# A Fourier-mixing and feed-forward kernel: three of the second batch's folds moved to GpSimd, and the last chunk's closing additions rearranged

## The chip, the cores and the metric

The kernel runs on one core of a Trainium2 chip. A core has a matrix engine (TensorE, "PE" in the profile, with its weight loads listed apart as "PEld"), an elementwise engine (VectorE, "DVE"), an activation engine (ScalarE, "ACT"), a programmable engine (GpSimd, "POOL") and a queue that issues transfers (SyncE, "SP"). The engines run side by side[...]. The metric is the time on the device in microseconds (us) of one execution, given as the median of several.

## The reference

```
X = fft(fft(x, axis=1), axis=2).real         # x: 8 batches x 3008 rows x 256 columns, f32
h = X.reshape(24064, 256) @ w_in             # 256 -> 2048
g = maximum(0.01 * h, h)                     # leaky ReLU
out = g @ w_out                              # 2048 -> 256
```

So a real part of a two-dimensional Fourier transform is taken for each of eight batches, and every one of its 24,064 rows then passes through a feed-forward layer with a leaky ReLU between its two matrices.

## The kernel before

**The Fourier part.** The transform along the 3008 rows is a matrix product with tables of cosines and sines, made small by folding: rows that the tables treat alike are added to or subtracted from one another first. The transform along the 256 columns is merged into the first matrix of the layer. The folds of a batch's `x` are `folds_of_x` (line 399) and `fold_halves_of_x` (line 413): elementwise additions in the tile `xt`. Of batch 1, `folds_of_x(0)` makes eight; then, on another part of the batch, `folds_of_x(1)` makes eight more and `fold_halves_of_x` the last eight. They are not run at once. They go into a queue (`Later`, line 937) and are let out one by one between the pieces of the matrix work.

**Folds by turns.** `by_turns` (line 952) treats every second fold alike. One of two first has ScalarE copy an operand to a PSUM bank (`dft_ps`, line 958), and VectorE then adds SBUF and PSUM (line 948). The other is an addition with both operands in SBUF, on VectorE as well (line 950); it alone is put on a list named `gate`. The next GpSimd addition waits for the last entry of that list (`wait_for_gate`, line 994). The additions of two SBUF results in `make` (line 1180) are put on it too.

**The layer.** After two pieces done in a plain way, the columns are worked in 31 chunks; the last of them, like most, has 376 columns in two halves of 188. For each chunk `up` (line 1094) makes 16 blocks of hidden values: two matmuls each, a ScalarE copy (line 1103), two VectorE operations (line 1110), and the leaky ReLU on ScalarE (line 1364 in the profile). The second matrix is applied by a fast matrix multiplication: 28 additions of hidden blocks (`sum`, line 1122, the operations of line 1127, 18 of them on GpSimd and 10 on VectorE), 26 block products (`product`, line 1133, the matmuls of line 1144), which gather in 24 sums numbered 0 to 23, and 34 additions of those sums (`make`, the operations of line 1188, all on VectorE) that give eight results. Each result is stored at once by `put` (line 1210, transfers of line 1213 on SP's queue).

**Banks.** The 24 sums of a chunk lie two to a PSUM bank, sum `a` in bank `a // 2`, and the banks rotate through three tiles, `sum_psa`, `sum_psb` and `sum_psc`. A bank is handed to `combine` (line 1153) when its second sum is complete. Sums listed in `COPIED` are copied to SBUF by ScalarE (line 1160); the others stay in PSUM until a `make` has read them. Before a bank is used again, `leave` (line 1172) issues the additions that still read it, so TensorE waits for VectorE there.

**The order of the work.** Each engine runs its instructions in the order in which the program issues them. That order comes from a list of events with due times, written out by hand (`rest`): up steps, sums, products, and between them the additions and folds that fit a budget of time for VectorE and GpSimd (`make_some`, `Later.emit`). What this listing decides is fixed before the program runs.

The additions of the last two sums of a chunk are these entries of the list `COMBINED`, by number of the value each makes (24 is the first entry): 25 = 20 + 22 by sign, 47 from 14 and 23, 35 from 25 and 32, and the results 44, 48 and 53 from those. In the last chunk sums 22 and 23 share `sum_psc`.

Of the kernel before, what the change touches and what calls it, by code (L numbers as in the profile page):

```python
# [82 lines left out]
COMBINED = [  # L83
    (0, 12, -1), (20, 22, -1), (1, 10, 1), (6, 9, 1), (14, 19, -1), (11, 26, -1), (15, 27, 1), (3, 7, 1), (18, 24, 1),
    (12, 29, 1), (8, 31, 1), (25, 32, 1), (28, 34, 1), (2, 7, 1), (36, 20, 1), (38, 21, 1), (6, 4, -1), (40, 33, -1),
    (30, 3, -1), (42, 17, -1), (43, 25, -1), (13, 33, -1), (45, 36, -1), (14, 23, 1), (47, 35, 1), (1, 5, 1), (49, 37, 1),
    (50, 27, 1), (37, 30, 1), (52, 35, -1), (26, 0, -1), (54, 13, 1), (55, 16, -1), (56, 28, -1),
]
RESULTS = [39, 41, 44, 46, 48, 51, 53, 57]
COPIED = [0, 1, 2, 3, 4, 6, 14, 20]  # L90
NA = 24

SUMS_AT = [14.51, 15.26, 16.05, 16.0, 16.74, 17.24, 17.74, 18.73, 18.48, 19.22, 19.47, 20.71, 20.32, 21.56, 22.06, 22.67, 22.04, 24.14, 24.64, 25.38, 25.37, 27.17, 27.22, 28.21, 29.08, 30.06, 30.17, 31.54]
UP_FROM, DOWN_FROM, PER_STEP = 1.20, 18.10, 6.5
ON_GPSIMD = (1, 2, 4, 5, 7, 10, 11, 13, 14, 15, 18, 19, 20, 22, 23, 24, 26, 27)
LAST_ON_POOL = ()
LAST_SOONER = 1.0
ON_POOL, ON_VECTOR, AHEAD, X_AHEAD, TRANSFORM_FROM, TURNS = 1.20, 1.20, 1, 2, 8, 2
SLOTS, RS, SS, PARTS = 28, 191, 764, 24
# [151 lines left out]
def chunks():  # L251

    plain, at = [], 0
    for j in range(PLAIN):
        plain.append((0, PARITIES[0], j * CW, CW, at))
        at += 2 * CW
    chunk = []
    for u, (b, c) in enumerate((b, c) for b in range(B) for c in PARITIES):
        for lo, hi in ((PLAIN * CW, UW[c]),) if u == 0 else ((0, KW[c]), (KW[c], UW[c])):
            n = (hi - lo + 1) // 2  # L260
            chunk.append((u, lo, hi - lo, n, at))
            at += 4 * n
    return plain, chunk, at
# [21 lines left out]
def tile_fnet_leaky_relu(  # L285
# [15 lines left out]
    nc = tc.nc  # L301
# [26 lines left out]
    def ring(tag):  # L328
        r = rings[tag]
        r[0] += 1  # L330
        return r[1][(r[0] - 1) % len(r[1])]
# [107 lines left out]
    class Rows:  # L439
# [3 lines left out]
        def __init__(self, src, scratch, part, c):  # L443
            self.src, self.scratch, self.part, self.c = src[0:ROWS], scratch, part, c
            self.places = PLACES[c] if part else range(16)
# [425 lines left out]
    blocks, chunk, _ = chunks()  # L871
# [65 lines left out]
    class Later:  # L937
# [2 lines left out]


        def __init__(self):
            self.queue, self.turn = [], 0

        def tensor_tensor(self, to, x, y, op):
            n = int(np.prod(to.shape[1:]))
# [5 lines left out]
        def by_turns(self, to, x, y, op):  # L952
            self.turn = (self.turn + 1) % TURNS
            if self.turn == 0:
                return self.tensor_tensor(to, x, y, op)
            n = int(np.prod(to.shape[1:]))
            copy = misc_ps[0 : to.shape[0], 0:n].rearrange("p (a b) -> p a b", a=to.shape[1])
            self.queue.append((0.0, None, lambda: nc.scalar.copy(copy, y)))
            self.tensor_tensor(to, x, copy, op)
# [34 lines left out]
    def wait_for_gate(ins):  # L994


        if gate:
            tc.add_manual_dep(ins.ins, gate[-1].ins.name,
                              mybir.DependencyInfo(mybir.DependencyClass.Sync, mybir.DependencyReason.DATA), reason="port")
            gate.clear()  # L1000

    class Slots:
# [29 lines left out]
        def place(self, i, n):  # L1032
            if i >= SLOTS:
                return block_sb[:, (i - SLOTS) * 4 * RF : (i - SLOTS + 1) * 4 * RF].rearrange("p (g n) -> p g n", g=4)[:, :, 0:n]
            return block_sb[:, i * SS : i * SS + 4 * RS].rearrange("p (g n) -> p g n", g=4)[:, :, 0:n]
# [37 lines left out]
    class Chunk:  # L1073
# [3 lines left out]
        def __init__(self, t):  # L1077
            self.u, self.j, self.m, self.n, self.first = chunk[t]
            self.w = 2 * self.n
            self.at, self.left = {}, uses_of_values()  # L1080
            self.sum_left = [0] * (NA + len(COMBINED))
            for x, y, _ in COMBINED:
                self.sum_left[x] += 1
                self.sum_left[y] += 1
            self.copy, self.bank, self.ready, self.held, self.open = {}, {}, set(), set(), []
# [36 lines left out]
        def sum(self, i, engine=None):  # L1122
# [7 lines left out]
            for s in free:  # L1130
                block.drop(s)

        def product(self, q, g):
            w, v, a = PRODUCTS[q]
            n = self.n
            bank, at = divmod(a, 2)
            if bank not in self.bank:
                self.bank[bank] = ring("sum")
                for part in every:
                    part.leave(self.bank[bank])  # L1140
            to = self.bank[bank][:, 256 * at : 256 * at + n]
            first = g == 0 and (q == 0 or PRODUCTS[q - 1][2] != a)
            last = q == len(PRODUCTS) - 1 or PRODUCTS[q + 1][2] != a
            nc.tensor.matmul(to, lhsT=weight(w)[:, g], rhs=self.value(v)[:, g],  # L1144
                             start=(first and at == 0), stop=(last and g == 3), skip_group_check=True)
            if g == 3:
                s = self.used(v)
                if s is not None:
                    block.drop(s)
                if last and (at == 1 or a == NA - 1):  # L1150
                    self.combine(bank)

        def combine(self, bank):

            n, here = self.n, [a for a in (2 * bank, 2 * bank + 1) if a < NA]
            for a in here:
                self.ready.add(a)
                if a in COPIED:
                    self.copy[a] = part_of.take()
                    nc.scalar.copy(part_of[self.copy[a]][:, 0:n], self.in_bank(a))  # L1160
                else:
                    self.held.add(a)
            for i, (x, y, _) in enumerate(COMBINED):
                v = NA + i
                if v not in self.ready and x in self.ready and y in self.ready:
                    self.ready.add(v)
                    self.open.append(v)

        def in_bank(self, a):
            return self.bank[a // 2][:, 256 * (a % 2) : 256 * (a % 2) + self.n]  # L1170

        def leave(self, bank):
            while any(self.bank[a // 2] is bank for a in self.held):
                self.make(self.open[0])

        def can_make(self, v):
            x, y, _ = COMBINED[v - NA]
            return all(s in self.copy or s in self.held for s in (x, y))

        def make(self, v):  # L1180

            x, y, sign = COMBINED[v - NA]
            self.open.remove(v)
            n = self.n
            xa, ya = (self.in_bank(s) if s in self.held else part_of[self.copy[s]][:, 0:n] for s in (x, y))
            self.copy[v] = part_of.take()
            in_sbuf = not (x in self.held or y in self.held)
            ins = nc.vector.tensor_tensor(part_of[self.copy[v]][:, 0:n], xa, ya, op=ALU.add if sign > 0 else ALU.subtract)  # L1188
            if in_sbuf:
                gate.append(ins)  # L1190
            for s in (x, y):
                self.sum_left[s] -= 1
                if self.sum_left[s] == 0:
                    if s in self.held:
                        self.held.remove(s)
                    else:
                        part_of.drop(self.copy[s])
            if v in RESULTS:
                self.put(v)

        def make_some(self, us):

            for v in list(self.open):
                x, y, _ = COMBINED[v - NA]
                pool = not (x in self.held or y in self.held)
                if us[pool] > 0 and self.can_make(v):
                    self.make(v)
                    us[pool] -= self.n / 960 + 0.07

        def put(self, v):  # L1210
            d, j = divmod(RESULTS.index(v), 4)
            n = self.n
            nc.sync.dma_start(out[d * P : (d + 1) * P, self.first + j * n : self.first + (j + 1) * n], part_of[self.copy[v]][:, 0:n])
            part_of.drop(self.copy[v])
# [61 lines left out]
    def rest():  # L1276
# [4 lines left out]
        for t in range(count):  # L1281
            for f in range(NF):
                events.append((16 * t + UP_FROM + f, 3, t, f))
            for i, s in enumerate(SUMS_AT):
                events.append((16 * t + (s if t < count - 1 else max(s - LAST_SOONER, min(s, 17.05))), 1, t, i))
            for m in range(4 * len(PRODUCTS)):
# [48 lines left out]
        for _, kind, t, i in events:  # L1335
# [13 lines left out]
            elif kind == 1:  # L1349
                every[t].sum(i, None if i in (LAST_ON_POOL if t == count - 1 else ON_GPSIMD) else nc.vector)  # L1350
            elif kind == 2:
# [66 lines left out]
    with tc.manual_schedule(engines={mybir.EngineType.DVE, mybir.EngineType.PE, mybir.EngineType.SP}):  # L1418
        with tc.manual_schedule(engines={mybir.EngineType.Pool, mybir.EngineType.Activation}):
# [9 lines left out]
            t = xt[:, 0 : 8 * FI * D].rearrange("p (h m c d) -> p h m c d", h=2, m=2, c=2 * FI)  # L1429
# [183 lines left out]
```

## Time and profile before

| | |
|---|---|
| median of 3 runs | 1825.97 us (1825.89 to 1826.29) |
| the profiled execution, its own time | 1826.21 us |
| its span, first to last instruction | 1824.4 us |
| TensorE busy | 1814.5 us (99% of the span) |
| VectorE busy | 1551.8 us (85%) |
| ScalarE, GpSimd busy | 1125.0 us, 1077.3 us |
| last matmul of the span | ends at 1819.58 us |
| last VectorE addition | ends at about 1821.3 us |

Positions are counted from the start of the span. A row of the timeline gives the start, the duration, the engine, the line, the operation with its output and input tiles, their sizes and a count; in brackets stands how long the engine had been idle before it, and what it waited for. A busy engine is not by itself the bound: what matters is which engine another one waits for at a given place. Rows of VectorE overlap a little at their ends[...]: two that are 0.99 us together start 0.46 us apart.

### The profile page before, as it was taken

To read this page: it belongs to the slowest core of one execution; us is meant where nothing else is said; L and a number is where in the kernel's file an instruction comes from. 1 tells how busy PE (TensorE), PEld (TensorE's weight loads), DVE (VectorE), ACT (ScalarE), POOL (GpSimd) and SP (SyncE) were. 2 spreads that over 40 slices of the span, in tenths; PEclk is the share of its full clock that TensorE was granted. 3 is DMA by queue.
4 is the path that set the end of the run, shared out by engine and by line. 5 is a ranking of instruction groups with operands and counts; after the bars stand their busy time and mean duration, and the time that the engine had idled before them with its cause. 6 is when DMAs were issued, how large, how long until landed. Compare 5 with 4: busy or idle time off the path is not lost.

```text
span 1824.4 us, 27085 instructions
## 1 busy us (share of the span) xinstructions
PE 1814.5 (99%) x9424; PEld 1543.8 (85%) x9424; DVE 1551.8 (85%) x3223; ACT 1125.0 (62%) x2298; POOL 1077.3 (59%) x584
## 2 busy tenths in 40 slices
PE   9999999999999999999999999999999999999998
PEld 7887888888888888888888888888888888888888
DVE  8979998897888978899787988879888798787678
ACT  4558666675666756566565666657666576665651
POOL 0244666565666665666665666656666666666660
PEclk9999999999999999999999999999999999999999
DMA  6312021202102021121101112010121100010000
GB/s 237 118 47 90 28 70 35 72 13 64 39 28 72 18 68 31 29 70 35 57 24 31 69 33 73 20 66 24 33 72 35 55 27 28 24 35 18 7 16 31
DMA packets 65897, 88.61 MB, mean 49 GB/s; under 512 B 10064, under 2 KB 53456, under 8 KB 65760
## 3 DMA queue, kind: packets, MB, share of 16 engines
q1 hardware_dynamic: 65616, 86.88, 14.6%
q8 instruction: 74, 1.21, 0.3%
q14 instruction: 63, 0.52, 0.1%
q10 hardware_dynamic: 144, 0.00, 0.0%
HBM read 62.12 MB, written 24.72 MB: 48 GB/s over the span
## 4 chain that ended last, share of the span: by engine, by line
PE 96%; DVE 3%; issue 0%; DMA 0%; ACT 0%; POOL 0%; DVEq 0%
PE sum_psc L1144 21%; PE sum_psa L1144 17%; PE sum_psb L1144 17%; PE cos_psa L1097 9%; PE sin_psa L1097 9%; PE sin_psb L1097 8%; PE cos_psb L1097 8%; PE dft_ps L703 3%; PE sum_psa L929 1%; PE dft_ps L929 1%; PE sum_psb L929 1%; PE sum_psc L929 1%; DVE block L1127 1%; DVE part L1188 0%; DVE block L1110 0%; PE sin_psb L891 0%
## 5 line engine op out<-in xcount | busy, mean ns | idle before, releaser
L1127 POOL TENSOR_TENSOR block<-block 128x752 f32<-128x752 f32 (+2 forms) x540 | 1045.6, 1948 | 615.3 <-DVE xt L950 173.4
L1364 ACT ACTIVATE block<-block 128x376 f32<-128x376 f32 (+5 forms) x718 | 426.6, 623 | 3.9 <-DVE block L1110 3.2
L1127 DVE TENSOR_TENSOR block<-block 128x752 f32<-128x752 f32 (+2 forms) x328 | 416.3, 1273 | 0.2
L1110 DVE TENSOR_TENSOR block<-cos,sin_psa 128x376 f32<-128x376 f32 (+2 forms) x510 | 250.9, 533 | 141.0 <-PE sin_psa L1097 137.4
L1144 PEld LDWEIGHTS sum_psc<-block,wt 128*128 128x128 f32 x1736 | 289.3, 189 | 47.1 <-issue 1.8
L1144 PE MATMUL sum_psc<-block,wt 128*128 128x188 f32 (+2 forms) x1736 | 327.2, 321 | 1.7 <-DVE part L1188 1.7
L1110 DVE TENSOR_TENSOR block<-cos,sin_psb 128x376 f32<-128x376 f32 (+2 forms) x482 | 240.1, 539 | 101.4 <-PE sin_psb L1097 100.3
L1144 PE MATMUL sum_psa<-block,wt 128*128 128x188 f32 (+2 forms) x1736 | 312.1, 321 | 0.0
L1144 PEld LDWEIGHTS sum_psa<-block,wt 128*128 128x128 f32 x1736 | 283.5, 189 | 22.8
L1103 ACT COPY cos<-cos_psa 128x376 f32<-128x376 f32 (+2 forms) x255 | 119.2, 467 | 249.3 <-PE cos_psa L1097 246.5
L1103 ACT COPY cos<-cos_psb 128x376 f32<-128x376 f32 (+2 forms) x241 | 113.8, 472 | 210.2 <-PE cos_psb L1097 210.1
L1097 PE MATMUL cos_psa<-mixc,wf 128*128 128x376 f32 (+2 forms) x510 | 199.8, 473 | 0.5 <-ACT cos_psa L1092 0.5
L1097 PE MATMUL sin_psa<-mixs,wf 128*128 128x376 f32 (+2 forms) x510 | 199.7, 473 | 0.0
L1188 DVE TENSOR_TENSOR part<-part 128x188 f32<-128x188 f32 (+2 forms) x465 | 188.9, 443 | 3.3 <-ACT part L1160 1.4
L1097 PE MATMUL sin_psb<-mixs,wf 128*128 128x376 f32 (+2 forms) x482 | 191.6, 479 | 0.0
L1097 PE MATMUL cos_psb<-mixc,wf 128*128 128x376 f32 (+2 forms) x482 | 191.4, 478 | 0.0
L1144 PE MATMUL sum_psb<-block,wo 128*128 128x188 f32 (+2 forms) x992 | 188.0, 321 | 0.0
L1144 PEld LDWEIGHTS sum_psb<-block,wo 128*128 128x128 f32 x992 | 165.2, 189 | 22.8
L1144 PEld LDWEIGHTS sum_psb<-block,wt 128*128 128x128 f32 x992 | 163.5, 189 | 22.8
L1144 PE MATMUL sum_psb<-block,wt 128*128 128x188 f32 (+2 forms) x992 | 176.9, 321 | 0.0
L1092 ACT ACTIVATE cos_psa<-nb,wn 128x376 f32<-128x376 f32 (+2 forms) x255 | 146.0, 573 | 8.5
L1097 PEld LDWEIGHTS sin_psa<-mixs,wf 128*128 128x128 f32 x510 | 96.5, 189 | 61.8 <-DVE block L1110 0.4
(212 smaller groups left out, 1953.3 us busy)
## 6 DMA issues: line engine op xcount, KB each, us to landing
xt<-in_x_dram SPq DMA_DIRECT2D x28, 1024.0 KB, 5.6
out_dram<-part SPq DMA_DIRECT2D x176, 94.0 KB, 1.7
out_dram<-part SPq DMA_DIRECT2D x64, 94.5 KB, 1.7
tabe<-in_seq_tab_dram SPq DMA_DIRECT2D x29, 190.0 KB, 2.5
nb<-nyq_dram SPq DMA_DIRECT2D x23, 188.0 KB, 3.8
block<-in_w_in_dram SPq DMA_DIRECT2D x8, 512.0 KB, 5.8
block<-in_w_out_dram SPq DMA_DIRECT2D x8, 512.0 KB, 4.5
xt<-in_first_x_dram SPq DMA_DIRECT2D x4, 768.0 KB, 8.4
```

What stands on the lines that cost most here:

```text
L703: nc.tensor.matmul(o, lhsT=still, rhs=moving, start=(i == 0), stop=(i == 3), skip_group_check=True)
L929: nc.tensor.matmul(sums[j][d][:, r * n : (r + 1) * n], lhsT=wo[:, fs[h] // 4, fs[h] % 4, d], rhs=a[r][h], start=(f == 0 and r == 0 and h = ...
L1092: nc.scalar.activation(cos_ps[self.half(f)][:, 0 : self.w], columns_of(nb_sb, self.u, self.j, self.w), ACT.Copy, scale=wn[:, f : f + 1])
L1097: nc.tensor.matmul(bank[:, 0 : self.w], lhsT=wf[:, i, f * P : (f + 1) * P], rhs=columns_of(mix_sb[i], self.u, self.j, self.w), start=(i == ...
L1103: nc.scalar.copy(copy, cos[:, 0 : self.w])
L1110: nc.vector.tensor_tensor(block.row(to, g, self.n), x, y, op=op)
L1127: ins = (engine or nc.gpsimd).tensor_tensor(self.value(16 + i), xa, ya, op=ALU.add if sign > 0 else ALU.subtract)
L1144: nc.tensor.matmul(to, lhsT=weight(w)[:, g], rhs=self.value(v)[:, g], start=(first and at == 0), stop=(last and g == 3), skip_group_check= ...
L1188: ins = nc.vector.tensor_tensor(part_of[self.copy[v]][:, 0:n], xa, ya, op=ALU.add if sign > 0 else ALU.subtract)
L1364: nc.scalar.activation(to, to, ACT.Lrelu)
```

## The change

Two things are changed, and they lie at opposite ends of the run.

First, in `by_turns` the additions with both operands in SBUF are counted. The seventh, eighth and ninth go to GpSimd, with a wait for the gate. The seventh and eighth are the two 128 x 4 x 127 folds of `folds_of_x(1)` that fill the upper columns; the ninth is the first 128 x 512 fold of `fold_halves_of_x`. They are put in the queue with a cost of zero, so the rest of the order stays as it was.

Second, the last chunk has its own list of additions, 37 in place of 34. Sum 23 gets a bank of its own (the next in the rotation, `sum_psa`), sum 22 is combined as soon as it is complete, and sum 20 is read from PSUM and no longer copied. The list is written so that sum 23 is used by one addition only, the one that gives the last result.

```diff
+LAST_COMBINED = [
...
+    (50, 27, -1), (14, 31, 1), (47, 31, -1), (41, 20, -1), (52, 20, 1), (53, 20, -1), (55, 22, -1), (54, 22, 1), (56, 22, 1),
+    (57, 23, 1),
+]
+LAST_RESULTS = [37, 39, 58, 43, 60, 46, 59, 51]
...
+X_ON_POOL = (7, 8, 9)
...
             if self.turn == 0:
+                self.alone += 1
+                if self.alone in X_ON_POOL:
+
+                    self.queue.append((0.0, True, lambda: wait_for_gate(nc.gpsimd.tensor_tensor(to, x, y, op=op))))
+                    return
                 return self.tensor_tensor(to, x, y, op)
...
+            self.last = t == len(chunk) - 1
+            self.combined, self.results = (LAST_COMBINED, LAST_RESULTS) if self.last else (COMBINED, RESULTS)
...
+        def place(self, a):
+
+            return (NA // 2, 0) if self.last and a == NA - 1 else divmod(a, 2)
...
-                if last and (at == 1 or a == NA - 1):
+                if last and (at == 1 or a >= (NA - 2 if self.last else NA - 1)):
                     self.combine(bank)
...
-                if a in COPIED:
+                if a in COPIED and not (self.last and a == 20):
                     self.copy[a] = part_of.take()
```

Elsewhere `COMBINED` becomes `self.combined` and `a // 2` becomes `self.place(a)[0]`. In the order of instructions of the changed kernel, VectorE loses the three folds; GpSimd has the first two of them after its thirteenth 128 x 500 addition of that stage, and the third after the fourteenth. At the end, TensorE's last four matmuls write `sum_psa` and no longer `sum_psc`, ScalarE loses its last copy, and VectorE's closing additions are five of two SBUF operands, five that read `sum_psb`, three that read `sum_psc` and one that reads `sum_psa`.

## The prediction

> **What bounds the kernel now.** I read the page's busy times and its chain first, then busy time in stretches of 20 us, then the timeline where TensorE is not full.
>
> ```profile
> PE 1814.5 (99%) x9424; PEld 1543.8 (85%) x9424; DVE 1551.8 (85%) x3223; ACT 1125.0 (62%) x2298; POOL 1077.3 (59%) x584
> ...
> PE 96%; DVE 3%; issue 0%; DMA 0%; ACT 0%; POOL 0%; DVEq 0%
> ```
>
> TensorE is the bound, and its work is not changed: as many matmuls of the same shapes. So a gain can come only from its idle time and from what follows its last matmul at 1819.58. The idle time is small, 1819.58 - 1814.5 = 5.1 us. By stretches it is 1.8 us before 40, 0.55 in 120 to 140, 2.21 in 180 to 200 and 0.5 in 1780 to 1800; none elsewhere. The change touches the third of these, and the tail.
>
> ```profile
> 160.00:180.00 20.00, 20.00 (x124) 15.90 (x123) 19.03 (x46) 15.38 (x29) 7.98 (x7) 1.00 0.03 7
> 180.00:200.00 20.00, 17.79 (x98) 14.66 (x98) 19.83 (x41) 14.79 (x37) 13.69 (x8) 1.00 0.10 29
> 200.00:220.00 20.00, 20.00 (x108) 17.36 (x108) 19.86 (x39) 13.27 (x27) 13.57 (x7) 1.00 0.11 30
> ```
>
> The columns after the length are PE, PEld, DVE, ACT and POOL. Around the idle time VectorE is full (19.0 to 19.9 of 20) and GpSimd is not. The timeline shows how VectorE came to be late:
>
> ```profile
> 163.50 1.66 DVE L950 TENSOR_TENSOR xt<-xt 128x508 f32<-128x508 f32 x1
> 167.19 0.67 DVE L950 TENSOR_TENSOR xt<-xt 128x508 f32<-128x508 f32 x1
> 170.60 0.69 DVE L950 TENSOR_TENSOR xt<-xt 128x512 f32<-128x512 f32 x1
> ...
> 174.58 1.25 POOL L1127 TENSOR_TENSOR block<-block 128x500 f32<-128x500 f32 x1 [1.88 <-DVE xt L950]
> 175.87 0.55 DVE L1110 TENSOR_TENSOR block<-cos,sin_psa 128x378 f32<-128x378 f32 x1 [0.90 <-POOL block L1127]
> 182.60 0.47 DVE L1188 TENSOR_TENSOR part<-part,sum_psc 128x125 f32<-128x125 f32 x2
> 183.22 0.90 PE L1144 MATMUL sum_psc<-block,wt 128*128 128x125 f32 x6 [1.66 <-DVE part L1188]
> 187.06 0.59 PE L1144 MATMUL sum_psa<-block,wo 128*128 128x189 f32 x2 [0.55 <-DVE part L1188]
> ```
>
> The first three rows are the folds that move. The two bracketed PE waits, 1.66 + 0.55 = 2.21 us, are the whole idle time of the stretch: TensorE needs a bank whose old sums VectorE has yet to read. The tail:
>
> ```profile
> 1817.46 0.36 DVE L1188 TENSOR_TENSOR part<-part 128x188 f32<-128x188 f32 x1 [1.41 <-ACT part L1160]
> ...
> 1819.62 0.61 DVE L1188 TENSOR_TENSOR part<-part,sum_psc 128x188 f32<-128x188 f32 x2 [1.34 <-PE sum_psc L1144]
> 1820.14 1.14 DVE L1188 TENSOR_TENSOR part<-part 128x188 f32<-128x188 f32 x4
> ...
> 1821.68 0.40 SPq L1213 DMA_DIRECT2D out_dram<-part  x1
> ```
>
> Six additions follow the last matmul, then the last of three stores, issued at 20.78, 21.21 and 21.68. From that issue to the end of the span are 2.70 us.
>
> **What the skill says.** "SBUF — State Buffer", Who interferes with whom: a VectorE operation with two SBUF inputs contends with a GpSimd one that reads SBUF; the one that came first blocks the other for its whole length; one SBUF input does not contend. The trace agrees: the fold at 163.50 met two GpSimd additions (162.24 to 164.61) and took 1.66 where its like takes 0.67. "GPSIMD Engine Reference", Elementwise — side-by-side cycle accounting: a float addition is 1.96 times slower there (2048 elements). The trace has 1.27 us for a GpSimd addition of 128x512 (line 665, at 103.92) against 0.69 on VectorE, 1.8 times.
>
> **Part one, the folds.** VectorE loses 1.66 + 0.67 + 0.69 = 3.02 us. GpSimd gains three additions of about 1.25 (its 128x500 rows have 1.16 to 1.27). I replay both queues on the clock of before.
> - After 163.50 VectorE's next pair (line 1110) started at 165.09, only because of the fold. Now it waits for its matmuls, which end at 164.12: start 164.16, gain 0.93, the rest is idle.
> - GpSimd's two additions end at 164.61; the first fold runs 164.6 to 165.85. The second waits by the gate for VectorE's addition of line 1188 (166.99 before, now 166.07 to 166.35), and then behind the addition of line 1127 (167.79, now 166.27 to 166.94): 166.95 to 168.2. The 128x500 addition queued behind it ends at 169.3 (before 169.78).
> - VectorE's SBUF addition of 170.40 would start at 169.02 but meets that one: 169.3, 0.3 lost. It is the gate of the third fold: 169.7 to 170.95. The next GpSimd addition ends at 172.2 (before 172.7), and holds the VectorE addition of 173.62 from 172.06 to 172.2.
> - The fold of 173.82 now ends at 173.1 (before 174.51), 1.4 earlier. It is the gate of the GpSimd addition of 174.58, which held VectorE until 175.87; now until 174.5. From there VectorE runs the same rows 1.4 earlier: the two readers of `sum_psc` at 181.2 in place of 182.60.
> - TensorE wanted that bank at 181.56 and got it at 183.22; now at about 181.8. The stall falls from 1.66 to 0.25.
>
> What is late next: TensorE's last product of this chunk needs GpSimd's second addition after the fold of 181.09. That row group (181.91, four in 7.29 us) starts 1.4 earlier, but its first two take 1.8 and 1.25 with a VectorE addition of 0.86 between, so the value is there at 184.5 where TensorE wants it at 184.05: 0.4 lost. The wait of 0.55 for `sum_psa` goes, since VectorE's readers of it then end at 184.5 and TensorE comes at 185.5. By 192 VectorE is about 1.2 ahead of before and TensorE, with no room over it there, cannot be more than 1.2 to 1.5 ahead. Stalls before 2.21, after about 0.9: **gain 1.3 us**. What comes later hides any rest, as TensorE has no idle time in 200 to 1780. ScalarE's copies that now wait for a fold on GpSimd are not reached before 167.4 and 170.1, after the folds' ends (165.85, 168.2). Queued GpSimd sums end no later than before, so none of their readers waits longer. No transfer moves.
>
> Bounds of this part: TensorE can win no more than its 2.21, and if all that VectorE gets is given back in blocking, it wins nothing. A loss is not excluded: see the last rival.
>
> **Part two, the tail.** Sum 22 is complete about 18.31 (eight matmul rows from 16.87) and its bank is read then, not after sum 23. The additions of sums 20 and 21 start at 17.07, since the ScalarE copy (17.11, 0.32) that VectorE waited 1.41 for is gone. Five at 0.26 from start to start, 0.38 for the one that reads its forerunner: 17.07, 17.45, 17.71, 17.97, 18.23. Then the three of sum 22 at 18.49, 18.75, 19.01 (ends 19.36), and the last at 19.62 to 19.97, 0.04 after the last matmul as before. Stores: 19.13, 19.56, and the last at 20.0 (0.43 apart as before), in place of 21.68. The 2.70 behind it stay: **gain 1.65 us**. TensorE needs `sum_psa` free at 18.14; its readers end at 15.14. Three more additions are in the sum; they lie under the last 16 matmul rows, without that cover they would be 3 x 0.26 = 0.8. Bounds 1.3 to 1.8.
>
> **Sum.** Span 1824.4 - 1.3 - 1.65 = 1821.45; own time of that execution 1826.21 - 2.95 = 1823.26. The median lies 0.24 under it: 1825.97 - 2.95 = **1823.0 us**, 0.16% less. A measurement can tell about 0.2%, 3.65 us, from no change, so I call this the same.
>
> **Rivals.**
> - *Only the tail gains* (blocking gives VectorE's time back). For: exclusive operations meet at 163.50, 183.72 and 187.96. Against: above only 0.45 us of new meetings. 1825.97 - 1.65 = 1824.3.
> - *The whole stall goes.* For: 3.02 us come off an engine late by 2.21. Against: 0.6 of it becomes idle time at once. 1825.97 - 2.2 - 1.65 = 1822.1, just beyond 0.2%.
> - *Slower: GpSimd becomes the bound.* The folds have 127-column rows that no GpSimd row of before shows. Between 164.6 and 175.9, where TensorE first wants the sum made at 174.58, there are three folds and three additions of 1.25: folds up to (11.3 - 3.75) / 3 = 2.5 us are covered. Beyond that TensorE waits 3 us for each us of fold price, less the 2.21 it waits already. At 6 us: 10.5 - 2.2 - 1.65 = 6.6 us slower, 1832.6; it takes 5 us to pass +0.2%. Against: 1.27 for the nearest row.
> - *The change does nothing* is excluded by the order: VectorE has three rows fewer, GpSimd three more.
>
> **Chances.** Forecast (gain 2.3 to 3.5) 0.55; only the tail, with a small loss or gain beside it, 0.27; whole stall 0.16; GpSimd bound 0.02. Leaving out under 1 in 10 on each side gives 1821.9 to 1824.9. Faster by over 0.2% is the whole stall, 0.16; slower 0.02; the rest 0.82.
>
> **What would show it.** Right: at 160 to 200 TensorE idles about 0.9 us, its wait before the `sum_psc` product is near 0.3; folds of 1.2 to 1.3 us on GpSimd; one VectorE addition after the last matmul and the last store 0.4 after it. Wrong: folds of 2 us or more; a wait of TensorE on GpSimd's line 1127 above 0.5; a VectorE SBUF row near 166 to 173 that takes 1.5; a first wait at some later place.

## The result and the profile after

The changed kernel takes 1822.87 us (1822.68 to 1823.44, 17 runs) against 1826.29 us (1825.89 to 1826.73, 17 runs) for the kernel before on the same chip: 3.42 us less, a ratio of 0.9982 with a 95% interval of 0.9975 to 0.9989. The profiled execution has a span of 1820.9 us and a time of its own of 1822.73 us. From the page, the busy times and the chain:

```profile
PE 1814.2 (100%) x9424; PEld 1543.4 (85%) x9424; DVE 1550.7 (85%) x3223; ACT 1124.1 (62%) x2297; POOL 1081.9 (59%) x587
...
PE 96%; DVE 2%; issue 0%; POOL 0%; DMA 0%; ACT 0%; DVEq 0%; POOLq 0%
```

TensorE's busy time is within 0.3 us of what it was; the span is shorter by 3.5 us, so what went is mostly time in which TensorE stood or was done. The stretches show the first place (columns: length, PE, PEld, DVE, ACT, POOL, then clock and transfers):

```profile
160.00:180.00 20.00, 20.00 (x123) 16.01 (x122) 18.16 (x45) 16.92 (x33) 11.78 (x10) 1.00 0.03 7
180.00:200.00 20.00, 19.14 (x108) 16.18 (x107) 19.85 (x44) 13.95 (x34) 15.08 (x8) 1.00 0.15 42
```

TensorE's idle time between 180 and 200 fell from 2.21 to 0.86 us, while VectorE is as full as before there (19.85 of 20). The timeline of the changed kernel around it, in which the additions of line 1188 before are now line 1210, those of 1127 now 1144, the folds of 950 now 960, and the folds on GpSimd are line 968:

```profile
164.38 1.27 POOL L968 TENSOR_TENSOR xt<-xt 128x508 f32<-128x508 f32 x1
...
166.35 1.58 POOL L968 TENSOR_TENSOR xt<-xt 128x508 f32<-128x508 f32 x1 [0.70 <-ACT block L1386]
...
169.47 1.28 POOL L968 TENSOR_TENSOR xt<-xt 128x512 f32<-128x512 f32 x1 [0.32 <-PE sin_psb L1114]
...
172.10 0.68 DVE L960 TENSOR_TENSOR xt<-xt 128x512 f32<-128x512 f32 x1
...
172.86 1.25 POOL L1144 TENSOR_TENSOR block<-block 128x500 f32<-128x500 f32 x1 [0.91 <-DVE xt L960]
...
174.14 0.55 DVE L1127 TENSOR_TENSOR block<-cos,sin_psa 128x378 f32<-128x378 f32 x1 [0.90 <-POOL block L1144]
...
178.50 0.94 DVE L1144 TENSOR_TENSOR block<-block 128x756 f32<-128x756 f32 x1
...
180.12 7.29 POOL L1144 TENSOR_TENSOR block<-block 128x756 f32<-128x756 f32 x4 [1.93 <-DVE xt L960]
...
180.88 0.47 DVE L1210 TENSOR_TENSOR part<-part,sum_psc 128x125 f32<-128x125 f32 x2
...
181.50 0.90 PE L1165 MATMUL sum_psc<-block,wt 128*128 128x125 f32 x6 [0.36 <-DVE part L1210]
...
181.95 1.98 DVE L1144 TENSOR_TENSOR block<-block 128x756 f32<-128x756 f32 x1
...
185.29 0.59 PE L1165 MATMUL sum_psa<-block,wo 128*128 128x189 f32 x2 [0.51 <-DVE part L1210]
```

The folds run on GpSimd in 1.27 to 1.58 us. The addition that stood at 174.58 now stands at 172.86, the two readers of `sum_psc` start at 180.88 in place of 182.60, and TensorE waits 0.36 us for that bank in place of 1.66. The wait for `sum_psa` is 0.51, where it was 0.55. The row at 181.95 matters below: one VectorE addition of 128x756 that takes 1.98 us, where one of the same shape at 178.50 takes 0.94. Here are the second and the third of GpSimd's four additions by themselves, then VectorE's row as it was in the kernel before:

```profile
181.87 1.25 POOL L1144 TENSOR_TENSOR block<-block 128x500 f32<-128x500 f32 x1
...
183.07 2.51 POOL L1144 TENSOR_TENSOR block<-block 128x756 f32<-128x756 f32 x1
```

```profile
183.72 1.97 DVE L1127 TENSOR_TENSOR block<-block 128x756 f32<-128x756 f32 x1
```

GpSimd's second starts 0.08 us before VectorE's row. VectorE's row ends 0.8 us after that second has ended (183.12), and the third takes 2.51 us where a GpSimd addition of this shape takes 1.80 at 188.78. So VectorE waited for the second and then went ahead of the third.

The tail of the changed kernel, from the timeline:

```profile
1815.30 1.52 DVE L1210 TENSOR_TENSOR part<-part,sum_psb 128x188 f32<-128x188 f32 x5 [0.49 <-PE sum_psb L1165]
...
1816.38 1.44 PE L1165 MATMUL sum_psa<-block,wo 128*128 128x188 f32 x8
1816.73 0.86 DVE L1210 TENSOR_TENSOR part<-part,sum_psc 128x188 f32<-128x188 f32 x3
...
1817.36 1.30 SPq L1235 DMA_DIRECT2D out_dram<-part  x3
...
1817.85 0.35 DVE L1210 TENSOR_TENSOR part<-part,sum_psa 128x188 f32<-128x188 f32 x1 [0.25 <-PE sum_psa L1165]
```

One addition follows the last matmul, and the third of the three stores is issued at 1818.27. From the end of the last matmul (1817.82) to the end of the span are 3.1 us; before they were 4.8.

A second, smaller gain stands at 179.77. First the kernel before, then the changed one:

```profile
179.77 0.30 PEld L1097 LDWEIGHTS sin_psb<-mixs,wf 128*128 128x128 f32 x2 [0.53 <-DVE block L1110]
...
180.51 1.05 PE L1144 MATMUL sum_psb<-block,wo 128*128 128x125 f32 x8
```

```profile
179.14 0.51 PEld L1114 LDWEIGHTS sin_psb<-mixs,wf 128*128 128x128 f32 x2
...
180.09 1.05 PE L1165 MATMUL sum_psb<-block,wo 128*128 128x125 f32 x8
```

Before, a weight load waits 0.53 us for VectorE's line 1110, whose row stood at 178.71 and stands at 176.99 in the changed kernel. The profile counts no idle time of TensorE there, but the rows behind come later: the same matmuls start 0.20 us earlier in the changed kernel at 175 and 0.42 us earlier at 180.5. This wait is in the timelines of the kernel before, of the tail alone and of the doubled folds, and in no other one below.

So the 3.5 us of span are 1.34 us of the two waits, some 0.23 of this hidden one, 1.7 of the tail, and 0.2 by which this execution was ahead at 158 us, before anything that was changed.

### The profile page after: what moved, and what is told of

It reads as the page before. It is cut to its first block, busy times and chain, and to the rows that moved or that the text cites. A ratio compares the mean times of both kernels' runs of the same rounds, so it can differ in the third digit from the quotient of the medians.

```text
span 1820.9 us, 27090 instructions
## 1 busy us (share of the span) xinstructions
PE 1814.2 (100%) x9424; PEld 1543.4 (85%) x9424; DVE 1550.7 (85%) x3223; ACT 1124.1 (62%) x2297; POOL 1081.9 (59%) x587
## 4 chain that ended last, share of the span: by engine, by line
PE 96%; DVE 2%; issue 0%; POOL 0%; DMA 0%; ACT 0%; DVEq 0%; POOLq 0%
PE sum_psc L1165 21%; PE sum_psa L1165 17%; PE sum_psb L1165 17%; PE cos_psa L1114 9%; PE sin_psa L1114 9%; PE sin_psb L1114 8%; PE cos_psb L1114 8%; PE dft_ps L713 3%; PE sum_psa L939 1%; PE sum_psb L939 1%; PE dft_ps L939 1%; PE sum_psc L939 1%; DVE block L1144 1%; PE sin_psb L901 0%; PE cos_psb L901 0%
```

## The experiments

All are variants of the changed kernel. Times are medians; "off before" is the distance to the kernel before, run beside each variant (1826.29 beside the change, 1826.18 to 1826.25 beside the others), and differences between variants below are differences of this column. The last two columns are TensorE's two waits near 182 and 185, from each kernel's timeline.

| variant | us | off before | ratio (95%) | wait for `sum_psc` | for `sum_psa` |
|---|---|---|---|---|---|
| the change | 1822.87 | 3.42 | 0.9982 (0.9975 to 0.9989) | 0.36 | 0.51 |
| folds only | 1824.58 | 1.60 | 0.9991 (0.9983 to 0.9999) | 0.36 | 0.50 |
| tail only | 1824.48 | 1.70 | 0.9991 (0.9984 to 0.9997) | 1.66 | 0.55 |
| the three folds left out | 1822.97 | 3.21 | 0.9982 (0.9975 to 0.9989) | 0.36 | 0.56 |
| each fold twice | 1825.75 | 0.43 | 0.9998 (0.9990 to 1.0006) | 1.66 | 0.50 |
| a fourth fold moved | 1823.22 | 2.97 | 0.9984 (0.9977 to 0.9991) | 0.55 | 0.51 |
| two folds moved | 1823.36 | 2.89 | 0.9984 (0.9978 to 0.9991) | 0.70 | 0.50 |
| two multiply-adds left out | 1822.95 | 3.30 | 0.9982 (0.9975 to 0.9989) | 0.36 | 0.50 |
| the tenth fold left out | 1822.27 | 3.98 | 0.9977 (0.9969 to 0.9986) | none | 0.50 |
| one sum back on VectorE | 1822.59 | 3.59 | 0.9980 (0.9972 to 0.9988) | none | 0.51 |
| bank only, old list | 1823.20 | 2.99 | 0.9983 (0.9976 to 0.9990) | 0.36 | 0.50 |
| list only, old bank | 1824.07 | 2.12 | 0.9988 (0.9981 to 0.9994) | 0.37 | 0.51 |

The intervals are wider than most of these differences, so a tenth or two between variants says nothing alone; the waits of the timelines, which repeat to a few hundredths, carry the readings.

**The two halves apart.** The folds alone (the last chunk keeps its old list):

```diff
-            self.last = t == len(chunk) - 1
+            self.last = False
```

> Only the three folds go to GpSimd; the last chunk is as before. Theory: the two parts are apart and add up, and the folds win TensorE's waits for banks between 160 and 200 us: 1.5 us (1.2 to 1.8) off the time of before, TensorE idle about 0.9 us in 180 to 200, and 4.8 us from the last matmul to the end of the span as before. Rival (the folds win nothing that lasts, the end is the tail's alone): within 0.3 us of before.

And the tail alone:

```diff
-X_ON_POOL = (7, 8, 9)
+X_ON_POOL = ()
```

> No fold goes to GpSimd; the last chunk is as changed. Theory: 1.7 us (1.4 to 2.0) off the time of before, 2.2 us of TensorE's idle time left in 180 to 200, and about 3.1 us from the last matmul to the end of the span. Rival (part of the tail's gain comes from the folds, since all that follows is earlier): under 1 us.

Measured are 1.60 and 1.70 us off, 3.30 together, against 3.42 for both. The halves add up, as halves at opposite ends of the run should, and the waits go with the folds alone: 0.36 and 0.50 in the first, 1.66 and 0.55 in the second. In the timeline of the folds alone the two waits lose 1.35 us together and the hidden one at 179.77 some 0.23, which is the 1.60 within the noise.

**What the folds still cost on GpSimd.** They are left out altogether, so that part of `xt` isn't folded, or each is made twice:

```diff
-                    self.queue.append((0.0, True, lambda: wait_for_gate(nc.gpsimd.tensor_tensor(to, x, y, op=op))))
```

> As changed, but the three folds are computed nowhere, so batch 1 is wrong in part; it bounds what taking them off VectorE can win. Theory: GpSimd's three additions block VectorE for 0.2 us in all, so leaving them out wins 0 to 0.4 us more than the change. Rival (what is left of TensorE's waits, 0.9 us, is GpSimd's blocking by the folds): 0.7 us or more beyond the change, and no wait of TensorE left in 180 to 200.

```diff
                     self.queue.append((0.0, True, lambda: wait_for_gate(nc.gpsimd.tensor_tensor(to, x, y, op=op))))
+                    self.queue.append((0.0, True, lambda: nc.gpsimd.tensor_tensor(to, x, y, op=op)))
```

> As changed, but each of the three folds is computed twice in a row on GpSimd (the second time to the same values), so a fold costs it about 2.5 us. Theory of the prediction: up to 2.5 us a fold is covered before TensorE wants the sum of the addition at 172.9, so the loss comes from VectorE blocked more often: 0.3 to 1.5 us slower than the change. Rival (GpSimd has no room): each further us of fold is a us of TensorE's wait, 3.5 us or more slower than the change, and so slower than before.

Without them the time is no lower (3.21 off before) and TensorE waits 0.36 and 0.56. Made once each, they cost nothing that can be measured, and what gains is that VectorE no longer makes them. Made twice, they cost 3.0 us, twice the upper end of what the theory gave and less than its rival. The timeline of this variant:

```profile
173.39 1.32 POOL L969 TENSOR_TENSOR xt<-xt 128x512 f32<-128x512 f32 x1
...
173.51 1.76 DVE L960 TENSOR_TENSOR xt<-xt 128x512 f32<-128x512 f32 x1
...
174.68 2.89 POOL L1145 TENSOR_TENSOR block<-block 128x500 f32<-128x500 f32 x2
...
176.42 1.91 PE L1166 MATMUL sum_psa<-block,wt 128*128 128x125 f32 x12 [0.78 <-POOL block L1145]
177.60 0.55 DVE L1128 TENSOR_TENSOR block<-cos,sin_psa 128x378 f32<-128x378 f32 x1 [1.88 <-POOL block L1145]
...
184.96 0.90 PE L1166 MATMUL sum_psc<-block,wt 128*128 128x125 f32 x6 [1.66 <-DVE part L1211]
```

The second execution of the third fold (173.39) blocks the tenth fold on VectorE (173.51, 1.76 us instead of 0.68). The tenth fold in turn blocks GpSimd's next addition: the two of 174.68 take 2.89 us, and two of 1.25 would take 2.5. TensorE waits for the first of the two (0.78 at 176.42) and VectorE for the second (1.88 at 177.60, where it was 0.90). The wait of 1.66 is back in full. So the room on GpSimd ends somewhere between one execution a fold (1.27 us) and two. What ends it is GpSimd's own queue, made longer by the blocking in both directions.

**One fold more, one fewer.**

```diff
-X_ON_POOL = (7, 8, 9)
+X_ON_POOL = (7, 8, 9, 11)
```

> As changed, with the eleventh fold on GpSimd too (the one that VectorE runs at 175.80, after its wait of 0.90 for GpSimd). What is left of the wait before the sum_psc product, 0.36 us, is lateness that VectorE gathers after 170. Theory: 0.6 us of VectorE's work less there ends that wait: 0.2 to 0.5 us faster than the change, with the wait of 0.5 before sum_psa left. Rival (TensorE's waits left over are set elsewhere): within 0.1 us of the change, or slower.

```diff
-X_ON_POOL = (7, 8, 9)
+X_ON_POOL = (7, 8)
```

> The seventh and eighth fold on GpSimd, the ninth on VectorE as before. Theory: VectorE is not ahead of TensorE by then, so each fold counts until it catches up at 169.47: the ninth is worth 0.3 to 0.7 us, and this is that much slower than the change. Rival (the first two folds alone bring all of the gain): within 0.15 us of the change.

By the times both are slower than the change, by 0.45 and by 0.53 us. The wait for `sum_psc` grows both times and accounts for 0.19 and 0.34 of it; the rest is no more than the noise (the variant without the folds, with the waits of the change, is 0.21 off as well). The gain that the theory of the fourth fold named is not there. With a fourth fold:

```profile
176.65 1.58 POOL L968 TENSOR_TENSOR xt<-xt 128x512 f32<-128x512 f32 x1 [1.92 <-DVE part L1210]
...
178.19 1.27 POOL L1144 TENSOR_TENSOR block<-block 128x500 f32<-128x500 f32 x1
...
178.52 1.74 DVE L1144 TENSOR_TENSOR block<-block 128x756 f32<-128x756 f32 x1
...
182.31 0.90 PE L1165 MATMUL sum_psc<-block,wt 128*128 128x125 f32 x6 [0.55 <-DVE part L1210]
```

The fold (176.65) and the GpSimd addition behind it (178.19) fill GpSimd up to 179.46, and VectorE's addition of 178.52 takes 1.74 us where it takes 0.94 in the changed kernel. The 0.68 us taken off VectorE come back as 0.80 of blocking. With only two moved, the ninth fold takes its 0.68 us on VectorE again, and TensorE waits 0.70 in place of 0.36. Three is the best number of the three tried.

**What VectorE is late by after 170.** The first variant drops two of the multiply-adds of line 978 from the queue (so part of `xt` isn't made):

```diff
+            self.rotated += 1
+            if self.rotated <= 2:
+                return
             n = int(np.prod(to.shape[1:]))
```

> As changed, but the first two multiply-adds of the second transform (0.59 us of VectorE, at 181.27 in the changed kernel) are left out, so that part of a batch is wrong. VectorE's addition of 128x756 then asks for the ports about 0.5 us before GpSimd's first addition ends, and no longer at its end. Theory (who waits at the end of the other's operation goes first): VectorE's addition runs between GpSimd's first and second, takes about 1.4 us with its wait and not 1.98, and TensorE's wait of 0.5 us before sum_psa ends; in its place TensorE may wait up to 0.4 us for GpSimd's second addition. Rival (GpSimd's queued operations follow one another without a gap): VectorE's addition waits for both, 2.3 us or more, and the wait before sum_psa stays at 0.4 us or more.

It took 1822.74 us (3.45 off before), but with two entries fewer the queue let all that followed out earlier, and TensorE runs a piece of the next transform (at 184.66) before the product for `sum_psa`. So it changes more than it was meant to and decides nothing. The second variant keeps their places in the queue, with nothing in them:

```diff
+            self.rotated += 1
+            if self.rotated <= 2:
+                self.queue.append((n / 960 + 0.1, False, lambda: None))
+                return
```

> As changed, but the first two multiply-adds of the second transform (0.59 us of VectorE, at 181.27 in the changed kernel) are left out with nothing else moved, so that part of a batch is wrong. VectorE's addition of 128x756 then asks for the ports about 0.5 us before GpSimd's first addition ends, and no longer at its end. Theory (who waits through the other's operation goes first when it ends; at 181.95 VectorE came too late for that): it takes about 1.4 us with its wait and not 1.98, and TensorE's wait of 0.51 before sum_psa ends; in its place TensorE may wait up to 0.4 us for GpSimd's second addition. Rival (GpSimd's queued operations follow one another without a gap): VectorE's addition waits for both, 2.4 us or more, and the wait before sum_psa stays at 0.4 us or more.

1822.95 us: no gain. The timeline of this variant shows where VectorE's freed time went:

```profile
180.40 7.27 POOL L1148 TENSOR_TENSOR block<-block 128x756 f32<-128x756 f32 x4 [1.93 <-DVE xt L960]
...
182.22 1.97 DVE L1148 TENSOR_TENSOR block<-block 128x756 f32<-128x756 f32 x1 [0.59 <-POOL block L1148]
...
185.56 0.59 PE L1169 MATMUL sum_psa<-block,wo 128*128 128x189 f32 x2 [0.50 <-DVE part L1214]
```

VectorE is now 0.59 us early and stands idle for it, because its addition at 182.22 writes a block that GpSimd's first of the four still reads. So it does not come early to the contention for SBUF ("the ports" of the expectation), and neither the 1.4 us of the theory nor the 2.4 of the rival is seen. GpSimd's first ends, VectorE is released, and GpSimd's second has already begun: VectorE's row takes 1.97 us again. The wait of 0.50 for `sum_psa` stays. So VectorE's load between 180 and 182 is not what this wait hangs on. In every trace but that of the first variant, the product that waits starts 5.15 to 5.17 us after GpSimd's group, so it hangs on the start of that group. No run moves the group's start alone, and what would end this wait stays open.

That group waits for a VectorE fold, and VectorE for GpSimd before it (0.90 us at 174.14 in the changed kernel). The next variant takes away the fold that opens this chain, the tenth, and keeps its place in the queue (again part of `xt` isn't folded):

```diff
+                if self.alone == 10:
+                    self.queue.append((int(np.prod(to.shape[1:])) / 960 + 0.13, True, lambda: None))
+                    return
```

> As changed, but the tenth fold (VectorE at 172.10) is left out, so batch 1 is wrong in part. It is the gate of the GpSimd addition for which VectorE waits 0.90 at 174.14. Theory (VectorE has caught up with TensorE at 169.47, and its lateness at the sum_psc product is made by the rows after that, which the change leaves): VectorE is 0.6 us earlier from there on, TensorE's wait before the sum_psc product falls from 0.36 to 0.1 or less, 0.2 to 0.5 us faster than the change. Rival (the wait left over is set by TensorE's or ScalarE's own order): the wait stays above 0.25.

It took 1822.27 us, 0.56 less than the change. Its timeline:

```profile
172.56 1.25 POOL L1147 TENSOR_TENSOR block<-block 128x500 f32<-128x500 f32 x1 [0.31 <-DVE part L1213]
...
173.84 0.55 DVE L1130 TENSOR_TENSOR block<-cos,sin_psa 128x378 f32<-128x378 f32 x1 [0.69 <-POOL block L1147]
...
179.83 7.28 POOL L1147 TENSOR_TENSOR block<-block 128x756 f32<-128x756 f32 x4 [1.94 <-DVE xt L960]
...
184.99 0.59 PE L1168 MATMUL sum_psa<-block,wo 128*128 128x189 f32 x2 [0.50 <-DVE part L1213]
```

The wait for `sum_psc` is gone; the 0.50 for `sum_psa` is not. So what was left of the first wait was made after 170, by the tenth fold and the GpSimd addition that it gates.

**A version from this.** In the changed kernel VectorE waits 0.90 us for the GpSimd addition at 172.86. Here it makes it itself:

```diff
-                every[t].sum(i, None if i in (LAST_ON_POOL if t == count - 1 else ON_GPSIMD) else nc.vector)
+                every[t].sum(i, None if i in (LAST_ON_POOL if t == count - 1 else ON_GPSIMD) and (t, i) != (0, 24) else nc.vector)
```

> The changed kernel, but in the second batch the first of the four sums that GpSimd makes after the tenth fold is made on VectorE, right behind that fold. Theory: VectorE, which in the changed kernel stood 0.90 us at 174.14 for exactly this addition of GpSimd's, makes it itself in 0.60 to 0.67 us, is 0.2 to 0.4 us earlier from there on, TensorE's wait before the third bank falls from 0.36 to 0.1 us or less, and the wait of 0.5 us before the first bank stays: 0.2 to 0.5 us faster than the change, about 1822.5 us. Rival: VectorE is the fuller engine of the two in this stretch, the 0.65 us comes on top of what it is late, or GpSimd's four longer sums only start earlier and hold it up elsewhere: within 0.1 us of the change, or slower by up to 0.5 us.

```profile
172.05 0.69 DVE L960 TENSOR_TENSOR xt<-xt 128x512 f32<-128x512 f32 x1
...
172.65 0.67 DVE L1144 TENSOR_TENSOR block<-block 128x500 f32<-128x500 f32 x1
...
173.24 1.00 DVE L1127 TENSOR_TENSOR block<-cos,sin_psa 128x378 f32<-128x378 f32 x2
...
180.42 0.47 DVE L1210 TENSOR_TENSOR part<-part,sum_psc 128x125 f32<-128x125 f32 x2
...
184.84 0.59 PE L1165 MATMUL sum_psa<-block,wo 128*128 128x189 f32 x2 [0.51 <-DVE part L1210]
```

The addition (172.65) follows the fold (172.05) without a gap, and the pair of line 1127 starts at 173.24 as one row, with no wait inside. The readers of `sum_psc` start at 180.42 in place of 180.88; TensorE does not wait for that bank at all, and is busy for 19.49 of the 20 us where it was busy for 19.14. The time is 1822.59 us (1822.28 to 1823.03), below both kernels, 0.17 us more off before than the change. By the timelines it is 0.35 us better; the times alone can't tell it from the change, as the intervals overlap.

**The tail's two edits.** The bank alone (old list, sum 20 copied as before):

```diff
-            self.combined, self.results = (LAST_COMBINED, LAST_RESULTS) if self.last else (COMBINED, RESULTS)
+            self.combined, self.results = COMBINED, RESULTS
...
-                if a in COPIED and not (self.last and a == 20):
+                if a in COPIED:
```

> The folds as changed; in the last chunk sum 23 has a bank of its own and sum 22 is combined when complete, but the additions are the old list and sum 20 is copied. Theory (the tail is a count of what must follow the last matmul): two additions that depend on each other follow it, and the last store goes out about 0.4 us later than with both edits: 2.8 to 3.1 us off the time of before. Rival (the new list is what gains): no more than 2.0 us off.

The list alone (sums 22 and 23 share their bank as before):

```diff
-            return (NA // 2, 0) if self.last and a == NA - 1 else divmod(a, 2)
+            return divmod(a, 2)
...
-                if last and (at == 1 or a >= (NA - 2 if self.last else NA - 1)):
+                if last and (at == 1 or a == NA - 1):
```

> The folds as changed; the last chunk has the new list and reads sum 20 in PSUM, but sums 22 and 23 share a bank as before. Theory: four additions follow the last matmul, and the last store goes out about 0.55 us earlier than before: 2.0 to 2.4 us off the time of before, folds included. Rival (the new list is what gains): 2.9 us or more off.

Against the folds alone (1.60 off before) the bank is worth 1.39 us and the list 0.52, and both 1.82. The timeline with the bank alone:

```profile
1815.34 0.32 ACT L1181 COPY part<-sum_psb 128x188 f32<-128x188 f32 x1 [7.37 <-PE sum_psb L1165]
1815.69 0.36 DVE L1210 TENSOR_TENSOR part<-part 128x188 f32<-128x188 f32 x1 [1.41 <-ACT part L1181]
...
1817.84 0.35 DVE L1210 TENSOR_TENSOR part<-part,sum_psa 128x188 f32<-128x188 f32 x1
1818.23 0.36 DVE L1210 TENSOR_TENSOR part<-part 128x188 f32<-128x188 f32 x1
```

and with the list alone:

```profile
1818.20 1.13 DVE L1210 TENSOR_TENSOR part<-part,sum_psc 128x188 f32<-128x188 f32 x4 [1.03 <-PE sum_psc L1165]
...
1818.84 1.30 SPq L1235 DMA_DIRECT2D out_dram<-part  x3
```

With the bank alone the copy and VectorE's wait of 1.41 for it are still there, but hidden: what remains is two additions after the last matmul, the second reading the first. With the list alone four remain, as `sum_psc` cannot be read until its second sum is complete. Counted after the last matmul there are six additions before, four with the list, two with the bank and one with both.

## Why the prediction was right, and where it was not

**The total.** The forecast was 1823.0 us, the same within 0.2%; measured are 1822.87 and 0.18% less. That is nearer than the sum behind it deserves, and in part luck: the forecast took 2.95 us off, the measurement gives 3.42, and the kernel before took 0.32 us more in this comparison than in the runs that the forecast started from. The tail came as foretold; the folds gained 1.6 us and not 1.3. The interval of the ratio also reaches past 0.2%, so "the same" held by little.

**The tail.** Foretold 1.65, measured 1.70 alone and 1.7 in the profile. Its steps held: five additions of the other bank, three of `sum_psc` under the last matmul rows, one of `sum_psa` behind them, and a last store about 0.45 us after the last matmul ended, with 2.7 us behind it. The three additional additions are hidden, as foretold.

**What the folds' sum left out.** TensorE's idle time was taken as span less busy time, so that TensorE could win no more than 2.21 us. The wait hidden in the busy time at 179.77 was put at nothing, and is some 0.23. The 0.9 of remaining waits was not a sum either: the waits that the working names are 0.25 and 0.4, which is 0.65, and 0.9 follows only from the bound that TensorE cannot get more than 1.2 to 1.5 us ahead. In the timelines both VectorE and TensorE are 1.6 us further ahead at 191 than at 158.

**The folds' price and the chain up to 181.** Foretold were three folds of about 1.25 us, starting at 164.6, 166.95 and 169.7; they took 1.27, 1.58 and 1.28 and started at 164.38, 166.35 and 169.47, in an execution that ran 0.2 us ahead. The idle time of VectorE after its first freed place, the tenth fold as the gate of the next GpSimd addition, and VectorE's wait of 0.90 behind that came as replayed. The forecast's 181.2 for the readers of `sum_psc` is 180.88 (181.1 with the 0.2), and its 0.25 for TensorE's wait is 0.36: on that clock the bank came 0.1 us earlier than foretold, but TensorE came 0.2 earlier, without its wait at 179.77. That 3.02 us off VectorE are worth no more is also as the working had it: the variant without the folds shows that even a free fold gives no more, because VectorE catches up with TensorE near 164 and 169.5, and what remains is made later, which the variants around the tenth fold confirm.

**What was late next: errors that cancelled.** The step "its first two take 1.8 and 1.25 with a VectorE addition of 0.86 between" failed. VectorE's addition did not get in between GpSimd's first two; it waited for the second, went ahead of the third and took 1.98. From this follow two errors. The foretold loss of 0.4 us on GpSimd's second addition is not there: TensorE doesn't wait for it. And the foretold gain of the 0.55 for `sum_psa` is not there either, since VectorE came to that bank's readers about as late relative to TensorE as before. Foretold were stalls of about 0.9 us in all, measured 0.36 + 0.51 = 0.87: right in sum, wrong in its parts. The variant with two multiply-adds left out shows the cause: VectorE is released only as GpSimd's first addition ends, and by then GpSimd's next has begun (181.87 against 181.95 in the changed kernel). The row was in the profile of before, at 183.72 with the same 1.97 us; the replay should have kept it and not put 0.86 in its place.

**The rivals.** "Only the tail gains" fell with the folds alone (1.60 off). "The whole stall goes" fell on the waits that stand, though 0.36 of it could be had with one more edit. "GpSimd becomes the bound" was right in kind and wrong in its point: the working gave folds up to 2.5 us for free, and the doubled folds, 2.6 to 2.9 us each, bring the whole wait back and give away 3.0 us. The working had 11.3 us for three folds and three additions of 1.25; there they take 12.6, from 165.00 to 177.57. A wait of 0.28 us before the second fold and the blocking by VectorE, which makes one of the additions 1.69 us long, had been put at nothing.

## What to carry to other kernels

When two engines wait for each other in turn, the room on the second one is not the free time in its queue: each instruction moved there can also block the first engine, as the fourth fold did, so try one more and one fewer, and look at the one wait that the move was to shorten. A row whose duration is twice that of its like is a fact of its place in the order; keep it in a replay unless the order itself changes. Span less busy time is not all the waiting of an engine: compare the starts of the same rows in both timelines as well. At the end of a run, count the instructions that must follow the last matmul: a bank for the last sum alone and a list that uses this sum once took them from six to one, and 1.7 us with them.

## What the runs showed of the hardware

- An addition of 128x512 with two SBUF operands takes 1.27 to 1.28 us on GpSimd and 0.68 on VectorE. The folds with 127-column rows (128x508) cost the same 1.27 where nothing blocks them, so their shape costs nothing extra.
- "SBUF — State Buffer" of the Trainium skill, Who interferes with whom, has the operation that came first block the other. The runs agree, and add what comes first when VectorE is released by the end of a GpSimd addition with another queued behind it: the queued one (begun at 181.87 in the changed kernel, VectorE's at 181.95), in every trace but that of the first multiply-add variant, where VectorE came later (1.97 to 1.98 us for a VectorE addition that takes 0.94 elsewhere). VectorE then goes ahead of the one after that, which takes 2.51 us in place of 1.80.
- A weight load's wait of 0.53 us for VectorE, at 179.77 before, shows as no idle time of TensorE; the two matmuls behind it show as 0.90 us in place of 0.80.
- The last three stores are issued 0.42 and 0.48 us apart, and the span ends 2.7 us after the last of them is issued; neither moved with the change.
